# Where the residual tiles of an attention loop are loaded from: the GpSimd queue instead of SyncE's, and one PSUM tile emptied in two copies

## The chip, the cores and the metric

The kernel runs on one core of a Trainium2 chip. The metric is the device time of one execution in microseconds (us). Before the change it is 821.57 us, the median of 3 runs (821.45 to 823.08). The profiled execution has a span of 820.0 us; all positions in time below are counted from the start of that span.

A core has these engines: TensorE (PE in the profile, matmuls; PEld are its weight loads), VectorE (DVE), ScalarE (ACT), GpSimd (POOL) and SyncE (SP). Transfers between DRAM and SBUF (the on-chip memory) run on 16 DMA engines that all queues share. SP, ACT and POOL can each issue transfers, and each works through its own instructions in order: an instruction that has to wait holds up everything behind it on the same engine.

## The reference: forward and backward of a small transformer block

`reference` returns the block's output and the gradients of six inputs. The block, cut to what matters here (S = 2048 rows, D = 640, H = 32 heads of 20, F = 1728):

```python
def _fwd_reference(A_x, A_wqkv, A_wo, B_x, B_w_gate, B_w_up, B_w_down):
    def _A_ref(x, wqkv, wo):            # linear attention
        ...                             # q, k, v = x @ wqkv; pq, pk = phi(q), phi(k)
        num = jnp.einsum("bhqd,bhde->bhqe", pq, kv)
        den = jnp.einsum("bhqd,bhd->bhq", pq, z)[..., None] + 1e-6
        o = num / den
        return (...) @ wo
    def _B_ref(x, w_gate, w_up, w_down):
        g = _silu(x @ w_gate)
        u = x @ w_up
        return (g * u) @ w_down
    x = A_x
    h = x + _A_ref(_layernorm(x, axis=-1), A_wqkv, A_wo)      # residual: x is needed again here
    h2 = h + _B_ref(_layernorm(h, axis=-1), B_w_gate, B_w_up, B_w_down)
    return h2
# reference(): jax.vjp of this with grad_out
```

The change touches only the line `h = x + ...`, which the kernel computes in a loop over 16 tiles of 128 rows, and a matmul of the backward pass (`dm`, the gradient of g*u, which is grad_out times w_down transposed) that is woven into the same stretch.

## The kernel before

The parts that matter, with cuts marked. `wk` gives a tile of 128 x 640 bf16 from a pool of 5 buffers, `mm` a PSUM tile of two banks from a pool of 4. All tiles of a pool take its buffers in turn. In the block below PE, DVE and SP keep the order of the text; ACT and POOL are put in order by the scheduler.

```python
def ln_rstd(mv, rstd, t0, nt, eng=nc.gpsimd):
    v = small.tile([P, 4], FP32, name="lnv", tag="lnv")
    eng.tensor_scalar(out=v[:, :nt], in0=mv[:, :nt, 1], scalar1=1e-5, ...)           # POOL
    nc.gpsimd.tensor_tensor(out=rstd[:, t0:t0 + nt], in0=v[:, :nt], in1=nhalf[:, :nt], op=ALU.pow)  # POOL
...
def dm_steps():                        # 24 steps, each of 10 matmuls and one eviction
    for g in (0, 1, 3):
        ...
        for t in range(0, ST, 2):
            ps = mm("ps_dm")
            dm_mm(ps, wdT3 if g == 3 else wdT, t, g)      # 5 matmuls into bank 0, then 5 into bank 1
            dst = dmst[:, t // 2] if g == 3 else dm_t[g][:, t:t + 2, :]
            nc.scalar.copy(out=dst[:, :, :w], in_=ps[:, :, :w])
            if g == 3:
                nc.scalar.dma_start(out=scr_dm_v[:, t:t + 2, :], in_=dst[:, :, :w])
            yield
...
def load_xr(t):
    if t < ST:
        xrs[t] = wk("xr")
        nc.sync.dma_start(out=xrs[t][:], in_=x_v[:, t, :])
...
    for t in range(3):
        load_xr(t)
    ...
    kv_blocks(KVT, "ps_kvt", ...)
    dm(1)                              # the step g == 0, t == 8
    for i in range(DT):                # the W2 blocks
        if i == 3:
            dm(1)
        ps = mm("ps_w2t")
        mm_heads(ps, ...)              # 7 matmuls
        nc.scalar.copy(out=half(W2T[:, i, :]), in_=row(ps))
        nc.sync.dma_start_transpose(out=W2[:, :, i * P:(i + 1) * P], in_=W2T[:, i, :])
    ...
    for t in range(ST + 2):            # the attention loop
        if t < ST:
            xr = xrs.pop(t)
            ps = mm("ps_a")
            mm_row(ps, ..., DT)                                                        # PE, 10 matmuls
            nc.vector.tensor_tensor(out=half(xr[:]), in0=row(ps), in1=half(xr[:]), op=ALU.add)  # DVE
            mv = small.tile([P, 4, 2], FP32, name="mv2", tag="mv2")
            ln_stats(xr[:], mv[:, 0, :])                                               # DVE
            ln_rstd(mv, rstd2, t, 1)                                                   # POOL
            h1s[t] = (xr, mv)
            dm(1)
        if t > 0:
            load_xr(t + 2)
        u = t - 2
        if u < 0:
            continue
        ...
        h1, mv = h1s.pop(u)
        nc.scalar.dma_start(out=scr_h1_v[:, u, :], in_=h1[:])
        nc.vector.tensor_scalar(out=hn[:, u, :], in0=h1[:], ...)                       # DVE
        nc.sync.dma_start_transpose(out=hnT[:, :, u * P:(u + 1) * P], in_=hn[:, u, :])
...
    for g in range(4):                 # the FFN stages; the first starts when the loop ends
        for t in range(0, ST, 2):
            # PE: pg, pu (10 matmuls each); ACT: sigmoid, sigmoid, copy, copy; DVE: 7 products and sums
            ...
        # then ps_dw: the weight gradients; its first group takes the last two tiles of m_s last
```

Of the kernel before, what the change touches and what calls it, by code (L numbers as in the profile page):

```python
# [20 lines left out]
def kernel(  # L21
# [8 lines left out]
    nc = tc.nc  # L30
# [18 lines left out]
    x_v = A_x.rearrange("b (t p) d -> p (b t) d", p=P)  # L49
# [13 lines left out]
    def mm(name):  # L63

        return psum.tile([P, 2, 512], FP32, name=name, tag="mm")
# [9 lines left out]
    def wk(name, w=D, pool=0):  # L75
        return wpools[pool].tile([P, w], BF16, name=name, tag="w", padded_shape=[P, D])
# [249 lines left out]
    with tc.manual_schedule(engines={EngineType.PE, EngineType.DVE, EngineType.Activation}):  # L326

        ps = mm("ps_warm")
# [37 lines left out]
        ps = mm("ps_z")  # L366
# [13 lines left out]
    def dm_mm(ps, wdT, t, g):  # L380
        w = GW[g]
        o = GM if g == 1 else 0
        for c in range(2):
            for kt in range(DT):
                nc.tensor.matmul(ps[:, c, :w], lhsT=dh2T[:, kt, (t + c) * P:(t + c + 1) * P],  # L385
                                 rhs=wdT[:, kt, o:o + w], start=(kt == 0), stop=(kt == DT - 1))

    def dm_steps():
        for g in (0, 1, 3):
            w = GW[g]  # L390
            if g == 1:
                dm_t[1] = big.tile([P, ST, GM], BF16, name="dm1", tag="B")
            elif g == 3:
                dmst = strips.tile([P, 8, 2, GM], BF16, name="dmst", tag="S")
            for t in range(0, ST, 2):
                ps = mm("ps_dm")
                dm_mm(ps, wdT3 if g == 3 else wdT, t, g)
                dst = dmst[:, t // 2] if g == 3 else dm_t[g][:, t:t + 2, :]
                nc.scalar.copy(out=dst[:, :, :w], in_=ps[:, :, :w])
                if g == 3:  # L400
                    nc.scalar.dma_start(out=scr_dm_v[:, t:t + 2, :], in_=dst[:, :, :w])
                yield

    dms = dm_steps()

    def dm(n):
# [42 lines left out]
    xrs = {}  # L449

    def load_xr(t):
        if t < ST:
            xrs[t] = wk("xr")
            nc.sync.dma_start(out=xrs[t][:], in_=x_v[:, t, :])

    with tc.manual_schedule(engines={EngineType.PE, EngineType.DVE, EngineType.SP}):
        yk = strips.tile([P, DT * D + HG * P], BF16, name="yk", tag="S")
# [4 lines left out]
        for i in range(DT):  # L462
            ps = mm("ps_y")
# [12 lines left out]
        for t in range(3):  # L476
            load_xr(t)
# [15 lines left out]
        for i in range(DT):  # L493
# [3 lines that stand above are left out]
# [11 lines left out]
        for t in range(ST + 2):  # L508
# [3 lines that stand above are left out]
                mm_row(ps, lambda i: pqsT[:, i, t * P:(t + 1) * P], lambda i, n0, n1: W2[:, i, n0:n1], DT)  # L512
                nc.vector.tensor_tensor(out=half(xr[:]), in0=row(ps), in1=half(xr[:]), op=ALU.add)
                mv = small.tile([P, 4, 2], FP32, name="mv2", tag="mv2")
                ln_stats(xr[:], mv[:, 0, :])
                ln_rstd(mv, rstd2, t, 1)
# [7 lines that stand above are left out]
            if u == 0:  # L524
                nc.sync.dma_start(out=scr_KVT.rearrange("(j p) c -> p j c", p=P), in_=KVT)
            if u == 2:
                nc.sync.dma_start(out=mat_v(scr_W2T), in_=W2T)
            h1, mv = h1s.pop(u)
            nc.scalar.dma_start(out=scr_h1_v[:, u, :], in_=h1[:])
            nc.vector.tensor_scalar(out=hn[:, u, :], in0=h1[:], scalar1=mv[:, 0, 0:1],  # L530
                                    scalar2=rstd2[:, u:u + 1], op0=ALU.subtract, op1=ALU.mult)
            nc.sync.dma_start_transpose(out=hnT[:, :, u * P:(u + 1) * P], in_=hn[:, u, :])


    with tc.manual_schedule(engines={EngineType.SP}):
# [13 lines left out]
        for g in range(4):  # L549
            w = GW[g]  # L550
# [112 lines left out]
    with tc.manual_schedule(engines={EngineType.SP, EngineType.Pool}):  # L663
# [18 lines left out]
        for t in range(ST + LAG_C):  # L682
            if t < ST:
# [6 lines left out]
                ps = mm("ps_dhn")  # L690
# [30 lines left out]
            ps = mm("ps_dp")  # L721
# [14 lines left out]
    with tc.manual_schedule(engines={EngineType.SP, EngineType.DVE}):  # L736
# [27 lines left out]
        for i in range(DT):  # L764
            ps = gts.pop(i, None)
            if ps is None:
                ps = mm("ps_gt")
# [25 lines left out]
        ps = ps_dz  # L793
# [18 lines left out]
        ps = mm("ps_dzb")  # L812
# [30 lines left out]
        for t in range(ST + LAG):  # L843
            if t in (2, 3):
                dwqk(0, t + 1, t + 2)
            if t < ST:
# [5 lines left out]
                ps = mm("ps_dk")  # L852
# [20 lines left out]
            ps = mm("ps_dxn")  # L873
# [131 lines left out]
```

## Time and profile before

| what | us |
|---|---|
| device time, median of 3 | 821.57 |
| span of the profiled execution | 820.0 |
| PE busy | 813.3 |
| attention loop on PE | 100.10 to 148.58 |
| first FFN stage on PE (pg, pu) | 148.58 to 178.85 |
| DVE waits for an `xr` load, 4 times | 9.5 in all |
| an `xr` load from issue to landing, median of 16 | 3.2 |

How to read it: the span is one execution. A busy PE is one that has a matmul running by the profile's model of their ends, so a few hundred nanoseconds between two groups of matmuls show only when the starts of the groups are compared with the length that such a group has elsewhere. A wait is named by the instruction that waited and by what ended the wait. Of the 16 `xr` loads (160 KB each) the first three are issued ahead of the loop and the others in it.

### The profile page before, as it was taken

The numbers are of one execution on the slowest core, as the hardware profiler recorded it, in microseconds if no ns is written. First come the engines' busy times: TensorE is split into PE (matmuls) and PEld (weight loads), VectorE is DVE, ScalarE is ACT, GpSimd is POOL, SyncE is SP. The second block draws the span as 40 slices with busy tenths as digits, with TensorE's granted clock in tenths as the row PEclk, the third lists the DMA queues.
The fourth block names the chain that finished last, engine by engine and source line by source line (L and its number), as shares of the span: only waits on it lengthen the run. The fifth ranks groups of instructions, "written<-read, shape, count | busy, mean of one in ns | idle before, by whom it ended". The sixth has DMA issues, their size and how long they took to land.

```text
span 820.0 us, 14053 instructions
## 1 busy us (share of the span) xinstructions
PE 813.3 (99%) x5540; PEld 521.0 (64%) x5540; DVE 442.9 (54%) x874; ACT 290.9 (35%) x412; POOL 187.6 (23%) x345
## 2 busy tenths in 40 slices
PE   8999999999999999999999999999999999999998
PEld 6776656555555555555566677777776777777675
DVE  6878776891087018810760147787884366631212
ACT  6982422770184126500741122322322133322010
POOL 3330022322412412221125311211210111112330
PEclk9999999999999999999999999999999999999999
DMA  9994589998769997894498757976498999899962
GB/s 297 186 343 113 140 174 281 307 204 176 191 126 209 203 224 160 185 245 115 106 237 171 256 139 217 222 205 166 116 216 171 170 167 187 167 198 272 222 176 76
DMA packets 278321, 158.61 MB, mean 193 GB/s; under 512 B 235052, under 2 KB 264877, under 8 KB 278256
## 3 DMA queue, kind: packets, MB, share of 16 engines
q1 hardware_dynamic: 251696, 82.12, 54.3%
q0 software_dynamic: 17744, 64.45, 25.8%
q10 hardware_dynamic: 8816, 11.16, 4.3%
q8 instruction: 43, 0.70, 0.4%
q14 instruction: 22, 0.18, 0.1%
HBM read 47.68 MB, written 53.66 MB: 124 GB/s over the span
## 4 chain that ended last, share of the span: by engine, by line
PE 82%; DVE 9%; ACT 3%; DMA 3%; issue 1%; SPq 1%; ACTq 0%; POOL 0%; DVEq 0%
PE ps_dw L627 21%; PE ps_dhn L109 14%; PE ps_dxn L877 8%; PE ps_o L937 7%; PE ps_dwqk L109 5%; PE pu L563 5%; PE pg L558 5%; PE ps_y L109 3%; PE ps_gt L678 3%; PE ps_dp L109 3%; PE ps_dk L109 3%; PE pdm L385 2%; DMA xr<-in_A_x_dram 2%; PE ps_dm L385 2%; DVE st L134 1%
## 5 line engine op out<-in xcount | busy, mean ns | idle before, releaser
L109 PE MATMUL ps_dhn<-wgT,cols 128*128 128x320 bf16 x864 | 119.5, 299 | 0.0
L627 PE MATMUL ps_dw<-dd,hn 128*128 128x448 bf16 (+1 forms) x640 | 118.8, 346 | 0.0
L109 PEld LDWEIGHTS <-cols 128*128 128x128 bf16 x864 | 84.5, 98 | 32.9
L627 PEld LDWEIGHTS <-hn 128*128 128x128 bf16 x640 | 62.6, 98 | 54.2
L629 DVE CAST dwev<-ps_dw 128x896 bf16<-128x896 f32 (+3 forms) x12 | 10.9, 907 | 122.9 <-PE ps_dw L627 122.9
L629 ACT CAST dwev<-ps_dw 128x896 bf16<-128x896 f32 (+1 forms) x20 | 17.6, 879 | 160.5 <-PE ps_dw L627 139.9
L592 POOL DMA_DIRECT2D scr_dT<-stg x64 | 34.7, 542 | 168.9 <-DMA stg<-dd 168.2
L147 DVE CUSTOM_DVE_ANT_0 lb_a<-lb_dy,hn 128x640 bf16<-128x640 bf16 x32 | 26.4, 825 | 75.4 <-ACT lb_dy L145 75.4
L563 PE MATMUL pu<-wgu,hnT 128*128 128x448 bf16 (+1 forms) x320 | 63.6, 346 | 0.0
L558 PE MATMUL pg<-wgu,hnT 128*128 128x448 bf16 (+1 forms) x320 | 63.6, 346 | 0.0
L937 PE MATMUL ps_o<-wd,mT 128*128 128x320 bf16 (+3 forms) x462 | 61.3, 295 | 0.0
L627 PE MATMUL ps_dw<-m_s,dh 128*128 128x448 bf16 (+1 forms) x320 | 60.5, 346 | 0.1
L877 PEld LDWEIGHTS <-ring 128*128 128x128 bf16 x480 | 47.0, 98 | 18.2
L937 PEld LDWEIGHTS <-mT 128*128 128x128 bf16 (+1 forms) x462 | 41.8, 97 | 17.6 <-issue 2.6
L877 PE MATMUL ps_dxn<-wqkvT,ring 128*128 128x320 bf16 x320 | 51.3, 299 | 0.0
L627 PEld LDWEIGHTS <-dh 128*128 128x128 bf16 x320 | 31.3, 98 | 27.4 <-issue 0.4
L563 PEld LDWEIGHTS <-hnT 128*128 128x128 bf16 x320 | 31.3, 98 | 27.1
L558 PEld LDWEIGHTS <-hnT 128*128 128x128 bf16 x320 | 31.3, 98 | 27.0
L298 PE MATMUL ps_kq<-wqk,xnT 128*128 128x320 bf16 x320 | 46.4, 299 | 1.0 <-ACT xnT L290 1.0
L385 PEld LDWEIGHTS <-dh2T 128*128 128x128 bf16 x320 | 31.1, 98 | 25.1 <-issue 0.2
L385 PE MATMUL ps_dm<-wdT,dh2T 128*128 128x448 bf16 (+1 forms) x240 | 46.9, 344 | 0.1
L145 ACT ACTIVATE lb_dy<-ps_dhn,rstd 128x640 bf16<-128x640 f32 x16 | 12.7, 793 | 85.5 <-PE ps_dhn L109 85.5
(162 smaller groups left out, 1277.1 us busy)
## 6 DMA issues: line engine op xcount, KB each, us to landing
scr_dT<-stg POOLq DMA_DIRECT2D x48, 224.0 KB, 3.3
cols<-scr_dT POOLq DMA_DIRECT2D x6, 1728.0 KB, 8.0
scr_m<-m_s POOLq DMA_DIRECT2D x12, 448.0 KB, 4.7
cols<-scr_dT ACTq DMA_DIRECT2D x2, 1728.0 KB, 9.5
out_dram<-dwev POOLq DMA_DIRECT2D x30, 112.0 KB, 3.4
scr_dT<-stg POOLq DMA_DIRECT2D x16, 192.0 KB, 2.6
scr_pk<-pk SPq DMA_DIRECT2D x4, 640.0 KB, 8.4
scr_pq<-pqa SPq DMA_DIRECT2D x4, 640.0 KB, 8.7
```

Source lines behind the costliest of these rows:

```text
L109: nc.tensor.matmul(ps[:, ci, :320], lhsT=lhs(k), rhs=rhs(k, *NCH[ci]), start=(start and k == 0), stop=(stop and k == n - 1))
L147: nc.vector.tensor_tensor_reduce(out=a[:], in0=dy[:], in1=xhat, scale=1.0, scalar=0.0, op0=ALU.mult, op1=ALU.add, accum_out=sums[:, 1:2])
L298: nc.tensor.matmul(ps[:, ci, :320], lhsT=xnT[:, t, k, :], rhs=wqk[:, k, w0 + n0:w0 + n1], start=(k == 0), stop=(k == DT - 1))
L385: nc.tensor.matmul(ps[:, c, :w], lhsT=dh2T[:, kt, (t + c) * P:(t + c + 1) * P], rhs=wdT[:, kt, o:o + w], start=(kt == 0), stop=(kt == DT - 1))
L558: nc.tensor.matmul(pg[:, c, :w], lhsT=hnT[:, kt, (t + c) * P:(t + c + 1) * P], rhs=wg[:, kt, 0:w], start=(kt == 0), stop=(kt == DT - 1))
L563: nc.tensor.matmul(pu[:, c, :w], lhsT=hnT[:, kt, (t + c) * P:(t + c + 1) * P], rhs=wg[:, kt, w:2 * w], start=(kt == 0), stop=(kt == DT - 1))
L592: nc.gpsimd.dma_start(out=scr_dT[t + c, :, KO[g]:KO[g] + GK[g], :], in_=stg[:, :GK[g], :])
L627: nc.tensor.matmul(ps[:, c, :w], lhsT=lhs(t), rhs=rhs(t), start=(t == 0), stop=(t == ST - 1))
L629: copy(out=ev[:, :len(parts), :w], in_=ps[:, :len(parts), :w])
L678: nc.tensor.matmul(ps[:, ci, :320], lhsT=dh1[:, t, i * P:(i + 1) * P], rhs=pqs_tm[:, t, n0:n1], start=(t == 0), stop=(t == ST - 1))
L877: nc.tensor.matmul(ps[:, ci, :320], lhsT=lhs[:, i, :], rhs=rhs[:, i, n0:n1], start=(k == 0 and i == 0), stop=(k == 2 and i == DT - 1))
L937: nc.tensor.matmul(po(t, ci), lhsT=mTs[t // 4][r, t % 4, j, :], rhs=wd[r, j, n0:n1], start=(t, ci) not in opened, stop=last)
```

## The change

All 16 loads of `xr` are issued by GpSimd instead of SyncE, and are kept at their place in the order of the text: on GpSimd, `load_xr(t + 2)` then stands behind the two small operations of `ln_rstd` of tile t. The loads leave SyncE's queue to the transposes and weight loads that share it. Second, the PSUM tile of the one `dm` step that stands directly ahead of the W2 blocks is emptied by two copies of one bank each instead of one copy of both; the aim is that the first bank can be emptied while the second is still being filled, and that the buffer is free sooner.

```diff
@@ dm_steps
-                nc.scalar.copy(out=dst[:, :, :w], in_=ps[:, :, :w])
+                if g == 0 and t == 8:
+                    for c in range(2):
+                        nc.scalar.copy(out=dst[:, c, :w], in_=ps[:, c, :w])
+                else:
+                    nc.scalar.copy(out=dst[:, :, :w], in_=ps[:, :, :w])
@@ load_xr
-            nc.sync.dma_start(out=xrs[t][:], in_=x_v[:, t, :])
+            tc.keep_in_program_order(nc.gpsimd.dma_start(out=xrs[t][:], in_=x_v[:, t, :]))
```

## The prediction

> **What bounds the kernel now.** I read the page first:
>
> ```profile
> span 820.0 us, 14053 instructions
> PE 813.3 (99%) x5540; PEld 521.0 (64%) x5540; DVE 442.9 (54%) x874; ACT 290.9 (35%) x412; POOL 187.6 (23%) x345
> ```
>
> PE is busy for all but 6.7 us, and most of that is the start. Nothing in the attention loop can win more than the short holes that it makes in PE. To find them I took PE's timeline from 84 to 190 us and subtracted the starts of neighbouring groups. In the loop a group ps_a takes 1.36 us and a dm group 1.89 us (448 columns) or 1.62 us (384 columns) from start to start. Three places are longer:
>
> ```profile
> 91.94 2.05 PE L385 MATMUL ps_dm<-wdT,dh2T 128*128 128x448 bf16 x10
> ...
> 114.49 2.06 PE L385 MATMUL ps_dm<-wdT,dh2T 128*128 128x448 bf16 x10
> 116.62 1.52 PE L109 MATMUL ps_a<-wvo,pqsT 128*128 128x320 bf16 x10
> ...
> 136.41 1.79 PE L385 MATMUL ps_dm<-wdT,dh2T 128*128 128x384 bf16 x10
> 138.28 1.52 PE L109 MATMUL ps_a<-wvo,pqsT 128*128 128x320 bf16 x10
> ...
> 178.85 6.52 PE L627 MATMUL ps_dw<-m_s,dh 128*128 128x448 bf16 x32
> ```
>
> 116.62 - 114.49 = 2.13 instead of 1.89: a hole of 0.24 us. 138.28 - 136.41 = 1.87 instead of 1.62: 0.25 us. The first ps_dw lasts 6.52 us where the later ones of its kind last 6.22: 0.30 us. A fourth hole is 0.10 us, ahead of 91.94 (the W2 group before it ends at 91.84). In sum 0.89 us.
>
> Next, what releases them. DVE's timeline:
>
> ```profile
> 115.75 0.82 DVE L513 TENSOR_TENSOR xr<-ps_a,xr 128x640 bf16<-128x640 f32 x1 [3.69 <-DMA xr<-in_A_x_dram]
> ...
> 137.40 0.82 DVE L513 TENSOR_TENSOR xr<-ps_a,xr 128x640 bf16<-128x640 f32 x1 [1.80 <-DMA xr<-in_A_x_dram]
> ...
> 149.65 0.82 DVE L513 TENSOR_TENSOR xr<-ps_a,xr 128x640 bf16<-128x640 f32 x1
> ```
>
> These are the residual adds of tiles 3, 10 and 15. The add frees its ps_a buffer. Four PSUM buffers are shared by ps_a and dm in turn, so ps_a(t) needs the add of tile t-2. Add 3 ends at 116.57, and ps_a(5) starts at 116.62; add 10 ends at 138.22, and ps_a(12) starts at 138.28. So both loop holes come from a late xr load. The chain of waits shows those loads, and how the third hole arises:
>
> ```profile
> 112.28 3.37 DMA xr<-in_A_x_dram
> ...
> 131.01 6.26 DMA xr<-in_A_x_dram
> ...
> 151.05 1.28 ACT L579
> ...
> 184.41 0.04 issue
> 184.45 5.65 PE ps_dw L627 x29
> ```
>
> ACT cannot begin the first FFN stage before it has issued the h1 store of tile 15, which waits for add 15 (149.65); its table load then starts at 151.05, and DVE starts at 154.90. From there DVE is full to 184 us (4.96 to 5.00 of each 5 us between 155 and 170, 4.93 of the last 5). A late add 15 is thus never made good: it moves the end of DVE's chain, and so ps_dw, one for one.
>
> **What the Trainium skill says.** "DMA: Bandwidth & Descriptors", section "Queues, rings and completion order", says that each DMA engine takes turns between the queue rows that have work, a packet at a time. That would let an xr load pass the bulk transfers queued on SP. The trace before agrees that SP's queue delays them: loads issued near the two wgu loads (560 KB each) took 5.5, 6.3 and 5.1 us, the others in the loop 2.4 to 4.6. The same page, "Issuing engines are not separate DMA queues", says that all queues run on the same 16 engines and that other issuers save only issue time. The trace: the DMA share is 1.04 to 1.15 from 120 to 152 us, so there is little free capacity to move to. "SBUF — State Buffer", section "SBUF: two separate sides", warns that some DVE operations keep GpSimd from writing descriptors; no run here shows that yet, and POOL's DMA instructions take their usual 0.54 us beside a busy DVE.
>
> **The change, part by part.**
>
> *The split eviction.* It removes one ACT copy of 896 columns and adds two of 448. The aim is to close the 0.10 us hole at 91.94, where that dm group waits for the buffer. But in the listing of the built program the copy of bank 0 carries the wait for the tenth matmul, the same as the single copy before, and the second carries none. Nothing starts earlier. ACT's 896-column evictions follow each other at 0.80 us and its 640-column ones at about 0.59, so a column costs 0.21 / 256 = 0.8 ns and an operation about 0.07 us besides. An extra operation lies on this short path: about **+0.05 us**.
>
> *The first three loads.* They go out on POOL behind the copies of E (52.20 to 54.02) instead of at 85 us. 480 KB more in a stretch whose DMA share is 1.03, with adds only at 106 us: **0**.
>
> *The loads in the loop.* SP loses 13 issues of about 0.57 us, which nothing on PE waits for. What matters is when each load may start. Before, SP issues load t+2 behind the transpose of hn(t-3). Now POOL issues it behind rstd(t). So a new chain arises: add(t), statistics, rstd(t), load(t+2), add(t+2). The distance from add to the end of rstd is read from tile 3:
>
> ```profile
> 117.82 0.30 POOL L139 TENSOR_SCALAR lnv<-mv 128x1 f32<-128x1 f32 x1 [5.04 <-DVE mv L135]
> 118.21 0.57 POOL L140 TENSOR_TENSOR rstd<-lnv,nhalf 128x1 f32<-128x1 f32 x1
> ```
>
> 118.78 - 115.75 = 3.03 us. From landing to add is 0.10 us (115.65 to 115.75). With L for the load from issue to landing, two tiles take 3.13 + L. PE needs 3.25 us a tile early and 2.98 late. Start: rstd(1) ends at 110.82, so with L = 2.7 add 3 comes at 113.6 instead of 115.75, and the hole at 116.62 goes. Six further hops of the odd tiles give
>
> add 15 = 113.6 + 6 x (3.13 + L) = 132.4 + 6 L.
>
> Break-even with 149.65 is at L = 2.88 us; every 0.1 us of L is worth 0.6 us. Below L = 2.74 all three holes close and PE itself sets the pace: -0.79 us. The new end is max(-0.79, 6 x (L - 2.88)) plus 0.05.
>
> *What L will be.* No load of this kind ran in this loop, so it is an estimate from loads of the same size on POOL's queue:
>
> ```profile
> xr<-in_A_x_dram SPq DMA_DIRECT2D x16, 160.0 KB, 3.2
> ...
> pkr<-scr_pk POOLq DMA_DIRECT2D x16, 160.0 KB, 4.0
> pqr<-scr_pq POOLq DMA_DIRECT2D x16, 160.0 KB, 2.6
> ```
>
> The pqr loads ran at a DMA share of about 0.7 (480 to 560 us), the pkr loads at about 1.0 (630 to 690), and most of those right behind another POOL transfer, which the xr loads would not be. The loop lies at 0.8 until 120 us and above 1.0 then. I take 2.7 early and 3.0 after: (2.7 + 5 x 3.0) / 6 = 2.95, which gives +0.4 us, with 0.05 on top: 822.0.
>
> **Rivals.**
> 1. *Pure gain.* Round-robin lets the loads overtake, L is about 2.6 as for pqr, DVE no longer waits for xr: 820.8. For it: 9.5 us of such waits vanish, and the loads at 127 to 134 us were slow behind wgu. Against it: PE had turned those 9.5 us into 0.49 us of holes, so little is to be had.
> 2. *The new chain becomes the bound.* L is 3.5 as in a full DMA: 6 x 0.62 = +3.7, that is 825.3; with 4.0, as pkr, 828. For it: DMA share above 1.0, and a look-ahead that shrinks. Against it: a slower loop also thins the DMA traffic, and pkr's figure is inflated by pairs.
> 3. *Nothing.* DVE keeps up with PE, and L settles where both forces meet: 821.5.
>
> **Range and chances.** The gain is floored at 0.8 us, the loss is open. Weights of about 0.45 for rival 1 or near it (820.9), 0.25 for no change (821.6), 0.3 for the chain (823 to 826) put the middle at 821.6. The range is 820.5 to 825.0. 2% are 16 us, more than any version of this: faster 0.005, same 0.985, slower 0.01.
>
> **What would show it.** DVE's waits on xr loads: gone, or more regular and every two tiles. The landing time of the xr loads on POOL against 2.88 us. Add 15 against 149.65. The first ps_dw: 6.22 us if rival 1 holds, longer than 6.52 if the chain bounds. The dm group behind the first W2 blocks: its hole stays at 0.10 us or grows. I would be wrong if POOL's own queue delays rstd, if hnT's transposes, now alone on SP, hold up the FFN stage, or if another engine's order shifts.

## The result: 8.7 us slower, and the profile after

In the same rounds the kernel before takes 822.33 us (median of 4 runs) and the changed kernel 831.08 us (830.37 to 832.33). The ratio is 1.0107, with a 95% interval of 1.0087 to 1.0127: about 1% slower, clear of the noise. The profiled span grew from 820.0 to 828.3 us. The page of the changed kernel:

```profile
span 828.3 us, 14065 instructions
PE 814.1 (98%) x5540; PEld 520.7 (63%) x5540; DVE 443.5 (54%) x874; ACT 291.0 (35%) x413; POOL 197.0 (24%) x361
```

PE's work is the same (814.1 us instead of 813.3), but PE now stands idle for 14.2 us instead of 6.7. POOL has 16 more instructions, the loads, and ACT one more, the second copy. Next, PE's timeline of the changed kernel (start, duration, group, and in brackets how long PE was idle before it and what ended that):

```profile
92.17 2.05 PE L385 MATMUL ps_dm<-wdT,dh2T 128*128 128x448 bf16 x10 [0.17 <-ACT dm L401]
...
134.17 1.52 PE L109 MATMUL ps_a<-wvo,pqsT 128*128 128x320 bf16 x10 [1.46 <-DVE xr L517]
138.53 1.52 PE L109 MATMUL ps_a<-wvo,pqsT 128*128 128x320 bf16 x10 [1.21 <-DVE xr L517]
...
145.27 1.52 PE L109 MATMUL ps_a<-wvo,pqsT 128*128 128x320 bf16 x10 [0.62 <-DVE xr L517]
...
163.22 2.05 PE L562 MATMUL pg<-wgu,hnT 128*128 128x448 bf16 x10 [2.15 <-ACT m_s L585]
...
189.41 3.19 PE L631 MATMUL ps_dw<-m_s,dh 128*128 128x448 bf16 x16 [1.07 <-DVE m_s L592]
```

Where there were two holes of a quarter microsecond in the loop, there are now five, of 0.2 to 1.5 us, each ended by a residual add (the three longest are shown). The FFN stage behind the loop has holes too, because the whole chain of ACT and DVE starts it late. The adds show by how much. These are adds 3, 9 and 15 in DVE's timeline of the changed kernel:

```profile
114.76 0.82 DVE L517 TENSOR_TENSOR xr<-ps_a,xr 128x640 bf16<-128x640 f32 x1 [2.47 <-DMA xr<-in_A_x_dram]
...
137.65 0.82 DVE L517 TENSOR_TENSOR xr<-ps_a,xr 128x640 bf16<-128x640 f32 x1 [2.06 <-PE ps_dm L385]
...
158.13 0.82 DVE L517 TENSOR_TENSOR xr<-ps_a,xr 128x640 bf16<-128x640 f32 x1 [1.85 <-issue]
```

Add 3 is 1.0 us earlier than before (115.75), add 15 is 8.48 us later (149.65). Between them the odd adds follow each other at (158.13 - 114.76) / 6 = 7.23 us, where PE could keep about 6.0.

The brackets of adds 9 and 15 name PE and "issue", not the load. They mislead. POOL's timeline of the changed kernel shows the load of tile 9 and what stands ahead of it; the answer of the transfers' view for a window that holds this issue alone gives its landing (the last column, us from issue):

```profile
130.23 0.29 POOL L139 TENSOR_SCALAR lnv<-mv 128x1 f32<-128x1 f32 x1 [0.90 <-DVE mv L135]
130.61 0.57 POOL L140 TENSOR_TENSOR rstd<-lnv,nhalf 128x1 f32<-128x1 f32 x1
131.14 0.63 POOL L458 DMA_DIRECT2D xr<-in_A_x_dram  x1
```

```profile
xr<-in_A_x_dram POOLq DMA_DIRECT2D x1, 160.0 KB, 6.4
```

131.14 + 6.4 = 137.5, and the add starts at 137.65: the load released it. The load itself was issued the moment rstd of tile 7 was done. This is the chain add, statistics, rstd, load, add that the prediction worked out, and it closes for every odd tile.

The 13 loads in the loop, tiles 3 to 15 in order, took 3.7, 3.2, 3.6, 5.7, 3.6, 4.5, 6.4, 3.4, 3.7, 4.5, 3.3, 3.5 and 4.2 us. At the end the chain of waits of the changed kernel reads:

```profile
158.13 0.84 DVE xr L517
158.99 0.33 ACTq L533
159.35 1.28 ACT L583
...
192.75 7.35 PE ps_dw L631 x38
```

It is the same path as before, later: the weight gradients are released at 192.75 instead of 184.45 us, 8.3 us, which is the whole difference of the spans (828.3 - 820.0).

### The profile page after: what moved, and what is told of

Read it like the earlier page. It is cut to its first block, busy times and chain, and to the rows that moved or that the text cites. A ratio compares the mean times of both kernels' runs of the same rounds, so it can differ in the third digit from the quotient of the medians.

```text
span 828.3 us, 14065 instructions
## 1 busy us (share of the span) xinstructions
PE 814.1 (98%) x5540; PEld 520.7 (63%) x5540; DVE 443.5 (54%) x874; ACT 291.0 (35%) x413; POOL 197.0 (24%) x361
## 4 chain that ended last, share of the span: by engine, by line
PE 87%; ACT 5%; DVE 5%; issue 2%; DMA 1%; POOL 0%; ACTq 0%; DVEq 0%
PE ps_dw L631 21%; PE ps_dhn L109 14%; PE ps_dxn L881 8%; PE ps_o L941 7%; PE pu L567 5%; PE pg L562 5%; PE ps_dwqk L109 5%; PE ps_dm L385 5%; PE ps_a L109 3%; PE ps_y L109 3%; PE ps_dk L109 3%; PE ps_gt L682 3%; PE ps_dp L109 3%; ACT phi_r L308 2%; PE pdm L385 2%
```

## The experiments

Ratios are to the kernel before in the same rounds, with 95% intervals. The diffs are against the kernel that each paragraph names.

### Each part of the change alone

The changed kernel, with the loads back on SyncE:

```diff
-            tc.keep_in_program_order(nc.gpsimd.dma_start(out=xrs[t][:], in_=x_v[:, t, :]))
+            nc.sync.dma_start(out=xrs[t][:], in_=x_v[:, t, :])
```

> The kernel before with the split eviction alone; all xr loads stay on SyncE's queue. If the split is beside the point, the time stays within 0.2 us of before (822.3 us in the same rounds), and the hole ahead of the dm group behind the first W2 blocks is 0.17 us, as in the changed kernel, instead of 0.10. If the split were the cause of the 8.7 us (a rival), it would be slower by several us here.

Measured: 822.16 us beside 822.06, ratio 1.0000 (0.9992 to 1.0009), and the hole is 0.17 us, as expected. The split eviction makes no difference to the time that can be seen.

The changed kernel with one copy instead of two, so that only the loads are moved:

```diff
-                if g == 0 and t == 8:
-                    for c in range(2):
-                        nc.scalar.copy(out=dst[:, c, :w], in_=ps[:, c, :w])
-                else:
-                    nc.scalar.copy(out=dst[:, :, :w], in_=ps[:, :, :w])
+                nc.scalar.copy(out=dst[:, :, :w], in_=ps[:, :, :w])
```

> The kernel before with the xr loads on GpSimd's queue in the order of the text; the eviction is one copy again. Both theories below expect the whole loss here: 830.9 to 831.1 us, add 15 near 158 us, the first ps_dw held up until about 192.6 us. A time near 822 would mean that the split and the queue act together.

Measured: 832.92 us, ratio 1.0121 (1.0100 to 1.0142), add 15 at 159.83. That is some 2 us more than expected; the interval overlaps that of the changed kernel. The loads are the whole loss.

### The place without the queue

The loads may cost because of where they now stand (behind rstd) or because of the queue that they use. The kernel before, loads still on SyncE, but each made to wait for rstd(t) as on GpSimd:

```diff
-            nc.sync.dma_start(out=xrs[t][:], in_=x_v[:, t, :])
+            d = nc.sync.dma_start(out=xrs[t][:], in_=x_v[:, t, :])
+            if last_rstd[0] is not None and t >= 3:
+                wait_for(last_rstd[0], [d])
...
-                ln_rstd(mv, rstd2, t, 1)
+                last_rstd[0] = ln_rstd(mv, rstd2, t, 1)
```

> The kernel before, loads on SyncE's queue, but each load from tile 3 on must wait for the rstd of the tile two ahead of it, as on GpSimd in the changed kernel. Theory A: slower than before by 2 to 8 us, as two tiles take 3.1 + L with SyncE's landing times of 3 to 4.5 us; add 15 comes at 152 to 158 us. Theory B: within 1 us of before, since the queue is the old one and its loads have the old landing times.

Measured: 827.31 us, ratio 1.0062 (1.0038 to 1.0085), as theory A had it. DVE's timeline of this kernel has add 15 here:

```profile
154.79 0.82 DVE L516 TENSOR_TENSOR xr<-ps_a,xr 128x640 bf16<-128x640 f32 x1 [1.09 <-PE pu L566]
```

So the place alone, with the old queue and the same bulk transfers beside it, brings 5.2 us of the loss. The loads landed in 2.3 to 5.6 us, 3.3 in the mean; on GpSimd the mean was 4.1. The other 3.3 us of add 15 (158.13 - 154.79) go with the queue.

### The bulk transfers in the loop, on either queue

The slow loads lie beside the 800 KB store of W2T and the first wgu loads (560 KB each). The next two kernels move these to the end of the loop (the weight loads behind the 14th transpose of hn, where the expectation says 15th). PE then waits for the weights, some 27 us, so the totals (852.69 and 852.50 us, one run each) are not comparable with anything; only the loop is read. First the loads on GpSimd, with one copy:

```diff
-            if u == 2:
+            if u == ST - 1:
                 nc.sync.dma_start(out=mat_v(scr_W2T), ...)
...
-        wgu = {0: load_wgu(0), 1: load_wgu(1)}
+        with tc.issue_after(late_hnT):      # the transpose of tile u == ST - 3
+            wgu = {0: load_wgu(0), 1: load_wgu(1)}
```

> The loads-only kernel (loads on GpSimd behind rstd of tile t), with the two bulk transfers of SyncE's queue moved out of the loop: the store of W2T to its end, the weight loads of the first FFN stage behind the 15th transpose of hn. The total is not comparable, as PE then waits for the weights. Looked at are the landing times of the xr loads and the pace of the adds. If the long landings (5.7 and 6.4 us in the changed kernel, against 3.2 to 3.6 elsewhere) come from the bulk transfers, no xr load issued between 110 and 150 us takes over 4.5 us, the median is 3.0 to 3.5, and add 15 comes at 151 to 153 us instead of 158. If the landing time is a property of the GpSimd queue in this loop whatever runs beside it, the median stays at 3.6 or more, single ones above 5 us remain, and add 15 stays near 158 us.

Then the same edit on the kernel whose SyncE loads wait for rstd:

> SyncE's loads made to wait for rstd(t), with the scr_W2T store and the first wgu loads moved out of the loop (the total is not comparable: PE waits for those weights). On GpSimd's queue in the same place without that bulk, L was 3.5 us in the median. Theory A (GpSimd's queue has a longer landing of its own): L on SyncE is 2.3 to 2.8 us in the median, add 15 at 149.5 to 151.5. Theory B (the queue makes no difference, the remaining traffic sets 3.5): L 3.3 to 3.7, add 15 at 154 to 155.

The transfers' view over the loop of the one on GpSimd, and add 15 in DVE's timeline:

```profile
xr<-in_A_x_dram POOLq DMA_DIRECT2D x13, 160.0 KB, 3.5
```

```profile
154.74 0.82 DVE L513 TENSOR_TENSOR xr<-ps_a,xr 128x640 bf16<-128x640 f32 x1 [1.01 <-issue]
```

The same two of the one on SyncE:

```profile
xr<-in_A_x_dram SPq DMA_DIRECT2D x13, 160.0 KB, 2.6
```

```profile
151.12 0.82 DVE L516 TENSOR_TENSOR xr<-ps_a,xr 128x640 bf16<-128x640 f32 x1 [1.44 <-DMA xr<-in_A_x_dram]
```

With the bulk away, the slowest load on GpSimd was 4.5 us instead of 6.4, but the usual one still took 3.5, and add 15 fell half way between what the two theories had said. In the same place and beside the same traffic, SyncE's loads took 2.6 in the median. So in this loop the GpSimd queue has about 0.9 us more from issue to landing (one execution each, on different chips, but 13 loads in each). Most of that lies ahead of the load's first packet. The instruction that issues a load of tile 14 on GpSimd and one of tile 7 on SyncE, in POOL's and SP's timelines:

```profile
147.79 0.63 POOL L454 DMA_DIRECT2D xr<-in_A_x_dram  x1
```

```profile
124.15 0.33 SPq L455 DMA_DIRECT2D xr<-in_A_x_dram  x1
```

GpSimd's queue has no packet until 149.5 and its first by 149.7, about 1.8 us after the issue; SyncE's has none until 125.1 and its first by 125.2, about 1.0 us after it. The longer instruction is 0.3 us of this gap. Most of the other loads differ as these two do.

Four kernels with the load behind rstd now stand side by side (L is the mean of the loads of tiles 5, 7, ... 15, a hop is (add 15 - add 3) / 6):

| queue, bulk in the loop | L | hop | hop - L | add 15 |
|---|---|---|---|---|
| SyncE, out | 2.8 | 5.97 | 3.2 | 151.12 |
| GpSimd, out | 3.6 | 6.67 | 3.1 | 154.74 |
| SyncE, in | 3.5 | 6.64 | 3.2 | 154.79 |
| GpSimd, in (the changed kernel) | 4.1 | 7.23 | 3.1 | 158.13 |

The column hop - L is the prediction's 3.13 us in every row, within 0.1 us. And the two causes add up: 3.6 us for the queue and 3.7 for the bulk, from 151.12, make 158.4, against 158.13. On SyncE with the bulk away, the place makes add 15 only 1.5 us later than in the kernel before (151.12 against 149.65).

### More look-ahead on GpSimd

Only the loads moved, but load t+2 is put ahead of tile t's work, so that it follows rstd(t-1) and has three tiles of time:

```diff
+            if t > 0:
+                load_xr(t + 2)
             if t < ST:
                 xr = xrs.pop(t)
...
-            if t > 0:
-                load_xr(t + 2)
             u = t - 2
```

> As the loads-only kernel, but the load of tile t+2 stands ahead of tile t in the text, so that on GpSimd it is behind the rstd of tile t-1 and not of tile t. Theory A (the chain add, statistics, rstd, load, add of the next tile but one sets the pace: 3.1 + L us for two tiles): the same chain now spans three tiles, so with a landing time L of 4.1 us it needs (3.1 + 4.1) / 3 = 2.4 us a tile against PE's 2.98 to 3.25, DVE keeps up, and the time is 821.5 to 822.3 us, as before or up to 0.8 us faster. Theory B (GpSimd's queue itself is the cause: its transfers land late or crowd out the others, whatever their place in the order): still slower than 827 us.

Measured: 824.27 us, ratio 1.0026 (1.0011 to 1.0042); the runs scatter from 821.5 to 830.4. Both expectations missed it. The look-ahead takes back most of the loss, not all. DVE's timeline of this kernel, adds 9, 10 and 15:

```profile
130.93 0.82 DVE L515 TENSOR_TENSOR xr<-ps_a,xr 128x640 bf16<-128x640 f32 x1 [0.68 <-PE ps_a L109]
137.09 0.82 DVE L515 TENSOR_TENSOR xr<-ps_a,xr 128x640 bf16<-128x640 f32 x1 [3.86 <-PE ps_a L109]
...
153.29 0.82 DVE L515 TENSOR_TENSOR xr<-ps_a,xr 128x640 bf16<-128x640 f32 x1 [3.23 <-PE pu L563]
```

From add 5 to add 9 PE sets the pace. Add 10 then comes 6.2 us after add 9: its load was issued at 127.96 just behind wgu, and the window that holds it alone says:

```profile
xr<-in_A_x_dram POOLq DMA_DIRECT2D x1, 160.0 KB, 9.1
```

127.96 + 9.1 = 137.1, the start of add 10. Again the bracket names PE. Add 15 waits in the same way for a load of 7.5 us.

The same with the bulk moved out of the loop (total 852.32 us, not comparable, one run):

> The load-ahead kernel (3 tiles of look-ahead on GpSimd's queue) with the same bulk transfers moved out. In the load-ahead kernel one load took 9 us beside the weight loads and add 10 came 3.9 us late. If the bulk is the cause: all loads of the loop land within 5 us, DVE waits for no xr load after add 4, the adds follow PE at 2.98 to 3.25 us a tile, and add 15 comes within 1.5 us of the end of its ps_a, near 148.5 to 150 us. If the queue is: adds 10 and 15 are again several us late.

```profile
147.17 0.82 DVE L515 TENSOR_TENSOR xr<-ps_a,xr 128x640 bf16<-128x640 f32 x1 [0.68 <-PE ps_a L109]
150.16 0.82 DVE L515 TENSOR_TENSOR xr<-ps_a,xr 128x640 bf16<-128x640 f32 x1 [0.68 <-PE ps_a L109]
```

These are adds 14 and 15 in DVE's timeline, 2.99 us apart as PE's pace wants. Loads of 2.9 to 5.7 us are hidden by three tiles of look-ahead; what the kernel with the bulk lost in the loop, it lost to the bulk. (Two loads went over the 5 us that had been expected, and it did not matter.)

### The old queue with more look-ahead

The kernel before, loads on SyncE, all one place earlier:

```diff
-        for t in range(3):
+        for t in range(5):
             load_xr(t)
...
-            if t > 0:
-                load_xr(t + 2)
...
+            load_xr(t + 3)
             nc.sync.dma_start_transpose(out=hnT[:, :, u * P:(u + 1) * P], in_=hn[:, u, :])
```

> The kernel before, loads on SyncE's queue; the first five are issued ahead of the loop, and load t+3 stands ahead of the transpose of hn(t-2) where load t+2 stood behind that of hn(t-3). Theory A (what counts is how many tiles a load may be in flight: here add(t), hn(t-2), load(t+3), so about 2.5 + L + 0.1 us for three tiles): with L up to 6 us that is 2.9 us a tile, DVE never falls behind, the holes of 0.24, 0.25 and 0.30 us close: 0.3 to 0.8 us faster than before. Theory B (SyncE's queue, shared with the transposes, is the limit, so the loads must leave it): no gain, as the loads still queue there; within 0.2 us of before or slower.

Measured: 821.62 us beside 822.27, ratio 0.9987 (0.9976 to 0.9998). It beats the changed kernel, and the kernel before by a little. PE's timeline of this kernel has the first weight gradients without a hole:

```profile
178.87 6.22 PE L626 MATMUL ps_dw<-m_s,dh 128*128 128x448 bf16 x32
```

and DVE's timeline has adds 10 and 15:

```profile
136.57 0.82 DVE L513 TENSOR_TENSOR xr<-ps_a,xr 128x640 bf16<-128x640 f32 x1 [3.36 <-DMA xr<-in_A_x_dram]
...
148.81 0.82 DVE L513 TENSOR_TENSOR xr<-ps_a,xr 128x640 bf16<-128x640 f32 x1 [0.68 <-PE ps_a L109]
```

The load of tile 10 took 9.2 us here too, beside the same wgu loads. Only that one add waits, and the adds are back at PE's pace by tile 15. The 0.79 us of holes that late loads had made (0.24 + 0.25 + 0.30) were all that the loads had to give. How much of it came is known only roughly: the medians differ by 0.65 us, the spans of the two profiled executions by 0.3, and the interval of the ratio covers 0.2 to 2.0.

The last kernel is this one with the loads on GpSimd:

```diff
-            nc.sync.dma_start(out=xrs[t][:], in_=x_v[:, t, :])
+            tc.keep_in_program_order(nc.gpsimd.dma_start(out=xrs[t][:], in_=x_v[:, t, :]))
```

> The kernel of the best placing (first five loads ahead of the loop, load t+3 ahead of the transpose of tile t-2), but on the GpSimd queue; the load then stands behind rstd(t), three tiles ahead of its use. Theory A (look-ahead decides, and a load on GpSimd still starts only after that tile's statistics): three tiles take 3.1 + L, so L may be up to about 5.8 us before PE's pace of 2.98 us a tile is missed; the loads beside the bulk take 9 us and delay one or two adds. Total 822.0 to 824.5 us, as the three-tile look-ahead on GpSimd gave 824.3; add 15 between 149 and 154. Theory B (the GpSimd queue itself costs, whatever the look-ahead): above 826 us. Theory C (the queue does not matter once the load stands early): 821.6 us as on SyncE, first ps_dw at 6.22 us.

Measured: 822.88 us beside 822.07, ratio 1.0009 (0.9999 to 1.0020); the interval touches 1, so slower than before is not shown, and no gain is. Theory B is out: the loss is nearly gone. The time lies in theory A's range, but in the profiled execution the loop looks as theory C had it: add 15 comes at 148.60, ahead of the 149 to 154 of theory A, and the first ps_dw lasts 6.22 us. That execution, at 825.80 us the slowest of 12, lost its time elsewhere, by a wait for one of the last transposes, as PE's timeline shows:

```profile
174.57 1.58 PE L557 MATMUL pg<-wgu,hnT 128*128 128x448 bf16 x5 [2.39 <-DMA hnT<-hn]
```

This hnT transpose, of tile 13, took 21.3 us from issue to landing here, and 14.2 with the loads on SyncE; other transfers of this stretch were slow too (an h1 store of 160 KB took 17.4). What slowed them was not tried, and it is one execution. So A and C are not told apart.

## Why the prediction was wrong

**The holes, and what makes them: right.** Giving the loads time closed the holes ahead of 116.62 and 138.28 and brought the first ps_dw to 6.22 us.

**The split eviction: right.** The hole ahead of 92.17 grew from 0.10 to 0.17 us where +0.05 was expected. Alone, the part changes nothing in the time that can be measured.

**The first three loads: right.** They went out at 54 us, took 8.7 us, and nothing waited for them.

**The new chain: right.** The hop is 3.13 + L in four kernels. A late add 15 passes on one for one: 8.48 us of add 15, 8.3 us of span. The first add came later than worked out, 114.76 instead of 113.6, because its load took 3.7 us instead of 2.7.

**What L will be: this step failed.** The prediction says "I take 2.7 early and 3.0 after: (2.7 + 5 x 3.0) / 6 = 2.95, which gives +0.4 us". The first load took 3.7 us and the six odd ones after it 4.13 in the mean. Six hops with L 1.18 us longer than 2.95 are 7.1 us, the late first add is 1.2 more, and 0.4 had been expected: together 8.7, against the 8.48 us by which add 15 came late. Put as one L of 4.1, the prediction's own line 132.4 + 6 L gives 157.0, against 158.13.

Two things were mis-sized in it. In this loop the GpSimd queue takes 0.9 us longer to land such a load than SyncE's, in the same place; I had 2.6 us for it from the pqr loads, a quieter stretch. And the loads did not pass the bulk on SyncE's queue: 5.7 and 6.4 us in the changed kernel, up to 9.5 with more look-ahead. The prediction had read the slow loads near wgu as a delay of SyncE's queue; they are slow on either queue. Not tested is the warning that it mentions, that VectorE's work keeps GpSimd from writing descriptors.

**The rivals.** Rival 2 is what happened, and its line "with 4.0, as pkr, 828" is the nearest number of the text (the profiled span moved by 8.3, the median by 8.7). Both arguments against it failed. The slower loop did thin the traffic (a DMA share of 0.82 to 1.08 from 120 to 152 us instead of 1.04 to 1.15), but the loads were not fast for it. And the pkr figure of 4.0, which was set aside, lies near what came (4.1), but that is luck: in the changed kernel the pkr loads themselves took 3.2 in the median. Rival 1 had the most weight because of round-robin between queues. "DMA: Bandwidth & Descriptors", section "Queues, rings and completion order", in the Trainium skill does say that the engines take turns, but nothing of it showed as protection here: 9.1 us on GpSimd's own queue beside wgu, 9.2 on SyncE's behind it. The range then cut this rival off: "the chain (823 to 826)" left out the 828 that stood a few lines above. The price of 0.6 us for every 0.1 us of L was known, and figures from 2.6 to 4.0 us lay on the table; the range should have gone up to 828 at least.

**The signs of being wrong.** Of the fears named at the end, rstd was not delayed by POOL's own queue: it starts 0.38 us after the operation ahead of it (130.23 to 130.61), as it did before (0.39, from 117.82 to 118.21). The transposes are seen to hold up the FFN stage only in the profiled execution of the last experiment.

## What to carry to other kernels

A load issued by an engine that also computes inherits that engine's order: look up which instruction stands ahead of it, draw the loop that this closes, and multiply a doubtful landing time by the number of hops before trusting its mean. If loads come late, give them more tiles of look-ahead in the queue that they are in; a second queue gave no way round the bulk. And where a wait is put down to an engine that had long been done, add up issue and landing of the transfers before believing it.

## What the runs showed of the hardware

- GpSimd's queue landed a 160 KB load later than SyncE's in this loop: 3.5 us in the median (3.3 to 4.5) against 2.6 (2.4 to 3.8), same place, same other transfers. "DMA: Bandwidth & Descriptors" in the Trainium skill, section "Specifications", has a first byte after about 1 us on GpSimd's path and 0.6 on SyncE's; the direction agrees, and the gap measured at landing is twice that. Part of the difference is the issuing instruction, 0.63 us against 0.33: counted from its end, the first packets of the two loads shown come after about 1.2 and 0.65 us, near the page's figures. Why the path to the first packet is longer on GpSimd's queue stays open.
- That page's fit for GpSimd transfers, in "Anatomy of one DMA — SWDGE (gpsimd) path", is 2.0 us plus bytes by 436 GB/s, which gives an estimate of 2.4 us for such a load; no load in the loop came under 2.9 on that queue, while the pqr loads in their quieter stretch took 2.6.
- POOL's instruction for each of these loads took 0.63 us in the loop, where the prediction had 0.54.
- Beside the wgu loads a load of 160 KB took 9.1 us on GpSimd's queue and 9.2 on SyncE's.
